# A fused attention and Fourier mixing kernel: column tiles, paired steps and folded tables on the Fourier side, one load a segment for the attention outputs, and a new order of the work

## The chip, the cores and the metric

The kernel runs on one core of a Trainium2 chip. The core has five engines with queues of their own: PE (TensorE, matrix multiplies, and PEld, its weight loads), DVE (VectorE), ACT (ScalarE), POOL (GpSimd) and SP (SyncE, which here only issues DMAs). PE reads SBUF and writes PSUM; ACT and DVE read PSUM; POOL does not in this kernel. Sixteen DMA engines move data between SBUF and HBM. The metric is the device time of one execution in microseconds, the median of several runs; less is better.

## What is computed

Two branches over the same x (2048 tokens, 640 columns, bf16), mixed by a gate per token:

```python
def _A_ref(x, wq, wk, wv, wo, beta):          # H = 32 heads of 20, 4 segments of 512
    ...
    for s in range(N):
        logits = jnp.einsum('bhqd,bhkd->bhqk', qs, ks) * scale + mask     # causal
        p = _softmax(logits, axis=-1)
        a_dot = jnp.einsum('bhqk,bhkd->bhqd', p, vs)
        pq = phi(qs)                           # phi(t) = t + 1 if t > 0 else exp(t)
        num = jnp.einsum('bhld,bhde->bhle', pq, M)
        den = jnp.einsum('bhld,bhd->bhl', pq, z)[..., None] + 1e-06
        o = g * (num / den) + (1.0 - g) * a_dot
        pk = phi(ks)
        M = M + jnp.einsum('bhld,bhle->bhde', pk, vs)
        z = z + jnp.einsum('bhld->bhd', pk)
    return o @ wo

def _B_ref(x, w_r, w_i):
    X = jnp.fft.rfft2(x.astype(jnp.float32), axes=(-2, -1))
    X = X * (w_r + 1j * w_i)
    return jnp.fft.irfft2(X, s=(S, D), axes=(-2, -1)).astype(jnp.bfloat16)

g = _sigmoid((x * gate_w).sum(-1, keepdims=True))
return g * a + (1 - g) * b
```

## The kernel before

**How it is put together.** `Kern.record` lists 2328 steps ("ops"), each with the buffers that it reads and writes, the engines that could run it, and a name. `Sched.schedule` then goes through `ORDER`, a tuple written out by hand in the file: every entry is twice a step's number, plus one if the step's second engine is to run it (for an eviction ACT first and DVE second, for an elementwise step DVE first and POOL second). Each engine's queue is the steps of that engine in this order. The durations and latencies in the class (`HOPS`, `COST`, `QUEUE`) serve to choose PSUM banks and DMA semaphores; at run time the engines are held only by semaphore waits, which `emit` derives from the steps' predecessors (`o.preds`) and from bank and semaphore reuse (`o.dyn`). SP's queue is in order: a DMA whose data isn't ready holds all behind it.

PSUM has eight banks: four for the logits (`qk`), taken together, and four (`gen`) for everything else.

**Attention side.** For each segment: xT is loaded transposed (`xt_load`, L883), q, k and v are projected, logits come in units for a pair of head groups (`qk_unit`, L1242), ACT takes the exponentials (L1278), POOL zeroes what lies above the diagonal (`mask`, L1296), and PE multiplies by v (`pv_flipped`, L1193, for segments 0 to 2; `pv_group`, L1304, for segment 3). For segments 0 to 2 the outputs go to a DRAM scratch `u_scr` and come back in `finish_tile` (L1522) as five loads `ld_u` of 128 KB a segment into `oU`; they are then multiplied by the reciprocal denominators (`normal`, which come back over `r_scr`), the memory part is added (`addmem`), and the output projection (`oproj`) runs in column tiles of 32 rows or in one piece, after whatever ran before on PE (`mode=-1`). Masks of one unit that belong to two groups are issued apart for each, 224 in all.

**Fourier side** (`fft`, L1381). The two-dimensional transform is written as matrix multiplies:

- `fold` (L906): x (16 tokens a partition) is folded along its 640 columns into even and odd halves, on DVE or POOL.
- F1: multiplies over the 128 partitions by `fcat`; the result `Ac` has 5 chunks of columns by 16 steps g of 128.
- For each step g: **D**, six matmuls with 128 columns of `Ac` as weights and the tables `big` streaming (161, 321 and 160 columns, twice), into two PSUM banks, evicted to `Bt` (`ev_D`). **T**: two banks of two matmuls each (tables `tt` as weights, 321 columns of `Bt` streaming). **W_mul** (L1455): DVE multiplies each bank with both parts of W into `Pt`, 642 elements. **W_add** (L1460): two adds of 321 elements make `Yt`, on DVE or POOL. **Tb**: six matmuls of 256 columns, weights `Yt`, into two banks, evicted to `Cp` (`ev_Tb`).
- Every second step, one load of 512 KB for `tt` and four of 80 KB for W (`ld_W`); both are double-buffered.
- **Db**: for each of 16 n2 and two types, three matmuls of 321 columns over `Cp`; one type is evicted to `eo` and the other added and subtracted by `sum_Db` (L1501) into `G`.

**End.** In `finish_tile`, for each tile of 128 tokens and each half of the columns, four matmuls by the gate table bring in `G` (`Fb`), `oproj` adds the attention part in the same bank, an eviction (`final`) and a store follow.

A matmul step has a tiling of the PE array, its `mode`: 0 is the whole array, 1 the logits' tiles (20 rows by 64 columns), 2 is four column tiles of 32 rows of output, which may stream different data, and -1 takes what stands. Matmuls are recorded on L529, or on L527 where an untiled one is split.

Of the kernel before, what the change touches and what calls it, by code (L numbers as in the profile page):

```python
# [8 lines left out]
ALU = mybir.AluOpType  # L9
# [6 lines left out]
H = 32  # L16
# [28 lines left out]
class Op:  # L45
    __slots__ = ("id", "alts", "preds", "succs", "prio", "banks", "nbytes", "npred", "eng", "t0", "t1",
                 "stamp", "need_inc", "dyn", "first", "outside", "name", "dma", "key", "xfer", "lock", "mode", "emode", "hold", "width")


class Sched:  # L50
# [6 lines left out]
    FREE, PORT, LATE = 52.0, (85.0, 55.0), 500.0  # L57
# [57 lines left out]
    COST = {(0, 1): 94.0, (0, 2): 94.0, (1, 0): 130.0, (1, 2): 130.0, (2, 0): 106.0, (2, 1): 100.0}  # L115

    def schedule(self, pools, order, nsem=56):
# [32 lines left out]
        two = False  # L150
# [24 lines left out]
        def head(e):  # L175
# [18 lines left out]
            if o.dma:  # L194
                gate = window()
                if gate is not None:
                    t = max(t, gate.t1 + self.HOPS[e]["dma"])
            if e == "dve" and o.lock:
                t = max(t, free["pool"] + (20.0 if two else -self.PORT[0]))
            elif e == "pool":  # L200
                t = max(t, port - self.PORT[1])
            return t

        while len(self.order) < len(order):
# [20 lines left out]
            free[e] = o.t1 = t + occ  # L225
            if e == "dve" and o.lock:
                port = t + occ
            if e == "pool":
                two = o.lock
            if o.dma:  # L230
                if o.hold:
                    free[e] = max(free[e], max(ring) + 170.0)
                for q in range(o.width):
                    ring[q] = max(ring[q], free[e] + 1300.0) + o.xfer
# [84 lines left out]
def make_tables():  # L319
# [12 lines left out]
    F, Fp = F.reshape(128, 128), Fp.reshape(128, 128)  # L332
# [20 lines left out]
    dd = np.arange(KD)  # L353
    IC = np.zeros((384, 322))
    IS = np.zeros((384, 322))
    IC[:KD, :KD] = ck[:, None] * np.cos(2 * pi * kd[:, None] * dd[None] / D)
    IS[:KD, :KD] = ck[:, None] * np.sin(2 * pi * kd[:, None] * dd[None] / D)
    IS[0] = 0
    IS[320] = 0
    IS[:, 320] = 0  # L360

    T = np.zeros((16, 128, 4, 128))
    Tp = np.zeros((16, 128, 2, 2, 16, 4, 2))
    n2 = np.arange(16)
    k2 = np.arange(16)
    for g in range(16):
        for half in range(2):
            for i in range(4):
                kb, pi_, kind, sg = pair_of(g, half, i)
                k = kb + 128 * k2  # L370
                ph = 2 * pi * np.outer(n2, k) / S
                c, s = np.cos(ph), np.sin(ph)
                m = half * 64 + k2 * 4 + i
                kr = n2 * 8 + pi_ * 2
                ki = kr + 1

                def put(t, rows, val):
                    T[g, rows[:, None], t, m[None, :]] = val
                if kind == "pair":
                    put(0, kr, c), put(0, ki, sg * s), put(1, kr, -s), put(1, ki, sg * c)  # L380
                    put(2, kr, -s), put(2, ki, sg * c), put(3, kr, -c), put(3, ki, -sg * s)
                else:
                    src = kr if kind == "zero" else ki
                    put(0, src, c), put(1, src, -s), put(2, src, -s), put(3, src, -c)

                def putp(r, typ, eo, val):
                    for q in range(16):
                        Tp[g, m[q], r, typ, :, pi_, eo] = val[:, q]
                if kind == "pair":
                    putp(0, 0, 0, c), putp(1, 0, 0, -s), putp(0, 0, 1, -sg * s), putp(1, 0, 1, -sg * c)  # L390
                    putp(0, 1, 0, -s), putp(1, 1, 0, -c), putp(0, 1, 1, -sg * c), putp(1, 1, 1, sg * s)
                else:
                    eo = 0 if kind == "zero" else 1
                    putp(0, 0, eo, c), putp(1, 0, eo, -s), putp(0, 1, eo, -s), putp(1, 1, eo, -c)

    def chunks(t):
        return np.ascontiguousarray(t.reshape(3, 128, -1).transpose(1, 0, 2))
    fcat = np.concatenate([F, np.eye(128), Fp], 1)
    inv = np.concatenate([chunks(IC), chunks(IS)], 1).reshape(128, 6 * 322)
    big = np.concatenate([dtab, inv], 1)  # L400
    hmask = np.zeros((128, 5, 8, VW))
    for t in range(5):
        for r in range(128):
# [3 lines left out]
            "tt": np.concatenate([T.reshape(16, 128, 512), Tp.reshape(16, 128, 512)], 2).astype(b),  # L407
            "hmask": hmask.reshape(128, 880).astype(b)}


def base_of(g, i):

    return (0, 32, 48, 16)[i] if g == 0 else (g, g + 32, 64 - g, 32 - g)[i]


def pair_of(g, half, i):

    if g == 0:
        if half == 0:
            return 32 * i, i % 2, ("zero", "pair", "nyq", "pair")[i], (1, 1, 1, -1)[i]  # L420
        return 16 + 32 * i, (3, 2, 2, 3)[i], "pair", (1, 1, -1, -1)[i]
    if half == 0:
        return g + 32 * i, i, "pair", (1, 1, -1, -1)[i]
    return 32 - g + 32 * i, 3 - i, "pair", (1, 1, -1, -1)[i]
# [48 lines left out]
class Kern:  # L473
# [10 lines left out]
    def b(self, *key):  # L484
        v = self.bufs.get(key)
        if v is None:
            v = self.bufs[key] = Buf(str(key))
        return v
# [23 lines left out]
    def mms(self, items, r, w, prio, name="", extra=0.0, mode=0):  # L512
# [18 lines left out]
        op = self.Sc.op({"pe": (f, cost, self.DRAIN.get(name, 141.0))}, r=r, w=w, prio=prio, name=name, mode=mode)  # L531
        return op
# [10 lines left out]
    def one(self, eng, fn, n, r, w, prio, per=None, fix=None, name="", after=()):  # L543
        fix0, per0, late = {"act": (65, 0.833, 110.0), "dve": (67, 1.04, 68.0), "pool": (132, 0.945, 50.0)}[eng]
        per = per0 if per is None else per
        fix = fix0 if fix is None else fix
        return self.Sc.op({eng: (fn, fix + per * n, late)}, r=r, w=w, prio=prio, name=name, after=after)
# [9 lines left out]
    def dma(self, dst, src, nbytes, r, w, prio, tr=False, name="", after=(), queue="sp"):  # L557
        def f(e):
# [3 lines left out]
            with self.nc.allow_non_contiguous_dma(reason="small strided loads"):  # L562
                return e.dma_start(d_, s_)
        cost, work, width = self.QUEUE[name] if name in self.QUEUE else self.QUEUE[name, nbytes]
        queues = ("sp", "act") if name in self.EARLY else (queue,)
        return self.Sc.op({e: (f, cost, 0.0) for e in queues}, r=r, w=w, prio=prio, nbytes=nbytes, name=name, after=after,
                          dma=True, xfer=work, hold=tr and nbytes > 500000, width=width)
# [3 lines left out]
        "ld_W": (620.0, 450.0, 16), "ld_beta": (400.0, 120.0, 16), "ld_big": (500.0, 2900.0, 16), "ld_den": (520.0, 150.0, 16),  # L571
        "ld_fcat": (400.0, 350.0, 16), "ld_g": (500.0, 1900.0, 16), "ld_gc": (580.0, 200.0, 16), "ld_gw": (420.0, 600.0, 16),
        "ld_hm": (600.0, 850.0, 16), "ld_r": (570.0, 700.0, 16), "ld_tt": (530.0, 1650.0, 16), "ld_u": (530.0, 600.0, 16),
        "ld_wka": (520.0, 1100.0, 16), "ld_wkb": (450.0, 1500.0, 16), "ld_wqa": (500.0, 1100.0, 16), "ld_wqb": (500.0, 2200.0, 16),
        "ld_wo": (600.0, 700.0, 16), "ld_wo2": (600.0, 3000.0, 16), "ld_wv": (450.0, 3000.0, 16), "ld_x": (450.0, 830.0, 16),
        "oT": (1300.0, 750.0, 16), "pad2": (370.0, 200.0, 10), "pad": (400.0, 1250.0, 10), ("pkT", 131072): (1260.0, 600.0, 16), ("pkT", 262144): (1280.0, 1100.0, 16),
# [1046 lines left out]
```

## Time and profile before

Three runs took 243.2, 249.15 and 241.87 us, median 243.2. The profiled execution took 240.85 us; its span, first to last instruction, is 238.9, and the remaining 1.95 lie around it. The granted PE clock is 0.998 on average.

| group of instructions | count | busy us | mean ns |
|---|---|---|---|
| ACT exponentials `ex<-psum` L1278 | 92 | 138.7 | 1508 |
| POOL masks `ex<-ex` L1299 | 224 | 122.0 | 567 |
| DVE W_mul `Pt<-psum,Wt` L1455 | 32 | 25.6 | 822 |
| PE D `psum<-big,Ac` | 96 | 18.1 | 258 |
| PE Db `psum<-big,Cp` | 96 | 18.0 | 302 |
| PE Tb `psum<-tt,Yt` | 96 | 16.5 | 276 |
| PE T `psum<-Bt,tt` | 64 | 13.3 | 302 |
| SP issues of W loads, 80 KB each | 32 | | |
| SP issues of `oU<-u_scr`, 128 KB each | 15 | | |

Busy time is the time in which at least one instruction of a group runs, and the mean is that of one instruction from start to end. Matmuls overlap, so for PE a group's busy time is far under count times mean, and the time from one matmul's start to the next is shorter still than the busy time suggests. DVE, ACT and POOL run one instruction after another, so there busy time is work.

### The profile page before, as it was taken

Reading aid. Unit: us, or ns where it says so; the run is one execution under the profiler, and the core shown is the slowest. Engines: PE = TensorE matmul, PEld = TensorE weight load, DVE = VectorE, ACT = ScalarE, POOL = GpSimd, SP = SyncE. Lnnn points to the kernel's source line nnn. Section 1 sums busy time; section 2 is a strip of 40 time slices with the busy share of each in tenths; the row PEclk is TensorE's granted clock in tenths of the full one; section 3 lists DMA queues with packets and bytes.
Section 4 is the critical chain, followed back from the end, with each engine's and each line's share of the span. In section 5 each row is a group of like instructions: output and inputs, shape, how many; then the busy total and the mean of one; then the engine's idle time right before and its main releaser. Section 6 shows DMA issues by size and latency. Waiting matters only on the chain.

```text
span 238.9 us, 10255 instructions
## 1 busy us (share of the span) xinstructions
PE 227.6 (95%) x4361; PEld 140.1 (59%) x4361; DVE 196.6 (82%) x481; ACT 199.5 (83%) x241; POOL 166.7 (70%) x297
## 2 busy tenths in 40 slices
PE   7899999999999999999989999999999999899994
PEld 2575566775456566555646655455645466567794
DVE  0579998889899996898999798997988896846563
ACT  2189688898899999999999979999899988797730
POOL 8523268457969956937974999875889868678730
PEclk9999999999999999999999999999999999999999
DMA  7999849996996876483779572364766995872223
GB/s 171 277 366 233 231 125 185 264 207 149 250 227 158 153 210 178 110 241 72 237 213 261 171 226 62 103 157 144 204 205 162 244 215 83 121 107 83 59 86 111
DMA packets 58928, 42.17 MB, mean 177 GB/s; under 512 B 30020, under 2 KB 55172, under 8 KB 58884
## 3 DMA queue, kind: packets, MB, share of 16 engines
q1 hardware_dynamic: 57844, 40.96, 69.9%
q8 instruction: 34, 0.56, 1.0%
q10 hardware_dynamic: 1040, 0.57, 0.8%
q14 instruction: 10, 0.08, 0.2%
HBM read 23.32 MB, written 12.30 MB: 149 GB/s over the span
## 4 chain that ended last, share of the span: by engine, by line
PE 54%; DVE 19%; ACT 14%; DMA 7%; issue 3%; SPq 1%; DVEq 0%
PE psum L529 48%; ACT ex L1278 9%; PE psum L527 6%; DVE Pt L1455 3%; DMA r_scr<-rc 3%; ACT et L1087 2%; DMA xT<-in_A_x_dram 2%; DMA Wt<-in_B_w_i_dram 2%; DVE xsb L921 2%; DVE xf L916 2%; DVE G L1501 1%; DVE va L1130 1%; DVE q L540 1%; DMA r<-r_scr 1%; DVE oU L1542 1%
## 5 line engine op out<-in xcount | busy, mean ns | idle before, releaser
L1278 ACT ACTIVATE ex<-psum 128x2048 bf16<-128x2048 f32 (+4 forms) x92 | 138.7, 1508 | 12.2 <-PE psum L529 10.1
L1299 POOL TENSOR_SCALAR_AFFINE_SELECT ex<-ex 128x256 bf16<-128x256 bf16 (+2 forms) x224 | 122.0, 567 | 37.2 <-ACT ex L1278 33.7
L529 PE MATMUL psum<-qkp 20*64 20x64 bf16 (+5 forms) x1280 | 32.3, 270 | 2.2 <-ACT ex L1278 2.0
L529 PE MATMUL psum<-xT,wk 128*128 128x256 bf16 (+1 forms) x280 | 33.9, 273 | 0.2
L529 PE MATMUL psum<-xT,wq 128*128 128x512 bf16 (+1 forms) x135 | 30.7, 380 | 0.8 <-DMA xT<-in_A_x_dram 0.8
L529 PE MATMUL psum<-wv,xT 128*32 128x321 bf16 (+3 forms) x400 | 30.0, 301 | 0.3 <-DVE va L1130 0.3
L1455 DVE TENSOR_TENSOR Pt<-psum,Wt 128x642 bf16<-128x642 f32 x32 | 25.6, 822 | 2.2 <-PE psum L529 1.9
L529 PEld LDWEIGHTS psum<-qkp 20*64 20x64 bf16 x1280 | 13.3, 102 | 19.7 <-ACT ex L1278 15.4
L529 PEld LDWEIGHTS psum<-xT,wk 128*128 128x128 bf16 (+1 forms) x280 | 19.9, 97 | 6.5 <-DMA wk<-in_A_wk_dram 0.6
L527 PE MATMUL psum<-wo,oU 128*32 128x320 bf16 x480 | 21.9, 300 | 0.7 <-DVE oU L1550 0.5
L921 POOL TENSOR_TENSOR xsb<-xf 128x320 bf16<-128x320 bf16 (+2 forms) x12 | 9.5, 790 | 16.1 <-DVE xsb L921 12.4
L529 PEld LDWEIGHTS psum<-wv,xT 128*32 128x32 bf16 (+1 forms) x400 | 14.6, 96 | 7.5 <-issue 2.6
L1130 DVE TENSOR_TENSOR va<-psum,ebx 128x320 bf16<-128x320 f32 x32 | 15.2, 484 | 4.4 <-ACT gate L1128 2.1
L529 PE MATMUL psum<-big,Ac 128*128 128x160 bf16 (+2 forms) x96 | 18.1, 258 | 0.4 <-DVE Pt L1455 0.3
L529 PE MATMUL psum<-big,Cp 128*128 128x321 bf16 (+1 forms) x96 | 18.0, 302 | 0.2 <-DVE G L1501 0.2
L529 PE MATMUL psum<-ex,va 128*32 128x64 bf16 (+3 forms) x576 | 17.4, 257 | 0.4 <-DVE mem L1175 0.2
L1501 DVE TENSOR_TENSOR G<-eo,psum 128x320 bf16<-128x320 f32 x32 | 14.7, 483 | 3.6 <-PE psum L529 2.6
L540 DVE CAST ot<-psum 128x320 bf16<-128x320 f32 x21 | 10.1, 491 | 9.1 <-PE psum L527 5.9
L529 PE MATMUL psum<-tt,Yt 128*128 128x256 bf16 (+1 forms) x96 | 16.5, 276 | 0.5 <-DVE Yt L1460 0.2
L529 PEld LDWEIGHTS psum<-ex,va 128*32 128x32 bf16 x576 | 10.8, 96 | 9.6 <-POOL ex L1299 1.3
L1087 ACT ACTIVATE et<-qu 128x512 bf16<-128x512 bf16 x25 | 15.6, 631 | 0.2
L527 PEld LDWEIGHTS psum<-wo,oU 128*32 128x32 bf16 x480 | 11.9, 96 | 5.4 <-issue 1.4
(99 smaller groups left out, 392.7 us busy)
## 6 DMA issues: line engine op xcount, KB each, us to landing
qkp<-qk_scr SPq DMA_DIRECT2D x28, 160.0 KB
tt<-tab_tt SPq DMA_DIRECT2D x8, 512.0 KB, 4.5
qk_scr<-qu SPq DMA_DIRECT2D x12, 256.0 KB, 3.1
u_scr<-ub SPq DMA_DIRECT2D x12, 256.0 KB, 3.7
xsb<-in_A_x_dram SPq DMA_DIRECT2D x8, 320.0 KB, 6.5
oU<-u_scr SPq DMA_DIRECT2D x15, 128.0 KB, 2.9
out_dram<-ot SPq DMA_DIRECT2D x12, 160.0 KB
Wt<-in_B_w_r_dram SPq DMA_DIRECT2D x16, 80.2 KB, 2.6
```

The source lines that it names most:

```text
L527: h = e.matmul(dst, wt, r_, start=st, stop=sp_, **{**kw, "tile_position": (0, q), "skip_group_check": True})
L529: h = e.matmul(o_, l_, r_, start=st, stop=sp_, **kw)
L540: alts["dve"] = (lambda e: e.tensor_copy(dst(), src()), 67 + 1.04 * n, 68.0)
L916: self.either(lambda e, r=r, op=op: e.tensor_tensor(xf.ap(r * 642, [321, 2], [1, 320]), xs.ap(o, [D, 2], [1, 320]), xs.ap(o + 320, [D, 2], ...
L921: self.either(lambda e, dst=dst, src=src, d0=d0, n=n, op=op: e.tensor_tensor(xs.ap(o + dst, [D, 2], [1, n]), xf.ap(src + d0, [321, 2], [1, ...
L1087: self.one("act", lambda e: e.activation(et.ap(0, [1, L]), qsl(), ACT.Exp), L, [qb], [b("et", pi_)], late, fix=95, name="phi_exp")
L1130: self.one("dve", lambda e: e.tensor_tensor(va.ap(i * H * VW + h0 * VW, [VW, nh], [1, DH]), self.ps(bank, 0, [DH, nh], [1, DH]), self.ebx. ...
L1278: self.one("act", lambda e, d=d, q=q: e.activation(self.ex.ap(*d), self.ps(bank, *q), ACT.Exp, scale=SC), n, [bank], [self.exb(s, 2 * pr + ...
L1299: self.one("pool", lambda e: e.affine_select(self.ex.ap(e0 + d0, [1280, 4], [1, n], np_=np_), self.ex.ap(e0 + s0, [1280, 4], [1, n], np_=np_),
L1455: self.one("dve", lambda e, ri=ri, Pt=Pt, Wt=Wt, wo_=wo_, bank=bank: e.tensor_tensor(Pt.ap(ri * 322, [644, 2], [1, KD]), self.ps(bank, 0, ...
L1501: self.one("dve", lambda e, q=q, n2=n2, bank=bank, eo=eo: e.tensor_tensor(self.G.ap(n2 * D + 639 * q, [1 - 2 * q, 320]), eo.ap(q, [1, 320] ...
L1542: self.either(lambda e, c=c: e.tensor_tensor(oT.ap(c * L, [1, L]), oT.ap(c * L, [1, L]), self.r4[s].ap(0, [1, L]), ALU.mult), L, [b("r4", ...
```

## The change

- **D** runs in column tiles (`mode=2`): one bank holds, for 64 columns of `Ac`, the cosine part in partitions 0 to 63 and the sine part in 64 to 127; a step still streams 1284 columns' worth over the four tiles, in 24 matmuls. `base_of`, `start_of` and `row_of` give the new order of the rows; `ev_F1` writes `Ac` in runs of 4.
- **T** contracts over all 128 rows at once, so one pass of 321 columns by four column tiles makes a bank, for two steps g together.
- **Steps in pairs**: eight pairs instead of sixteen steps. `W_add` takes 642 elements; `Z_fold` is new: it adds and subtracts the mirrored halves of `Yt` into `Zt` (644 and 640 elements, one operand read backwards). `Pt` and `Yt` are single-buffered, `Zt` double.
- **Tb** works with 64 rows for each step of a pair, in two row tiles (`mode=3`, new), 128 columns a matmul, into two banks.
- **Folded tables**: `Db` streams 161, 321 and 160 columns instead of three times 321, and `sum_Db` writes every second element. `big` shrinks from 805 to 644 KB and each `tt` load from 512 to 256 KB. W comes in 8 loads of 40 KB a pair.
- **Loads**: x in 4 loads of 640 KB instead of 8 of 320; xT of segments 1 to 3 in three pieces; `oU` in one load of 640 KB a segment, with 5 KB in a row, and `wo` rows in the matching order.
- **Masks** of the two groups of a unit are joined where their buffers lie next to each other: 33 fewer.
- **Order**: `ORDER` is replaced, and 2328 steps become 2293. In `Sched`, the durations of DMAs, the fetching of PE's instructions and the port that DVE and POOL share are modelled otherwise; of this only one line adds waits: a POOL step waits for the locked DVE step that stands ahead of it.

The core of the diff:

```diff
@@ Sched.schedule
             if e == "dve" and o.lock:
                 port = t + occ
+                ldv = o
             if e == "pool":
-                two = o.lock
+                if ldv is not None:
+                    o.dyn.append(ldv)
+                two, ldv = o.lock, None
...
+D_PARTS = (((0, 160, 161, 0), (1, 0, KD, 162), (2, 0, 160, 484)), ((2, 0, 160, 644), (3, 0, KD, 804), (4, 160, 161, 1126)))
+DB_PARTS = (((0, 0, 161, 0), (1, 0, KD, 162), (2, 161, 160, 484)), ((0, 161, 160, 644), (1, 0, KD, 804), (2, 0, 161, 1126)))
...
+def start_of(g, X, h):
+
+    return ((0, 32), (16, 48))[X][h] if g == 0 else ((g, 64 - g), (g + 32, 32 - g))[X][h]
...
@@ fft
-        for g in range(16):
...
+        for pr in range(8):
...
+            for r, wd in enumerate((self.wr_d, self.wi_d)):
+                for h in range(4):
+                    row, row1 = (start_of(2 * pr + h // 2, X, h % 2) for X in range(2))
...
+            for g in (2 * pr, 2 * pr + 1):
+                Bt = self.Bt[g % 2]
+                for X in range(2):
+                    bank = Bank(1, "gen")
...
+                    for n_, parts in enumerate(zip(*D_PARTS)):
+                        items = []
+                        for h in range(4):
+                            def th(h=h, n_=n_, part=parts[h // 2], g=g, X=X, bank=bank):
+                                c, c0, n, tc = part
+                                return (self.ps(bank, c0, [1, n], p0=32 * h, np_=32), self.Ac.ap(c * 2048 + g * P + X * 64 + h % 2 * 32, [1, 32]), big.ap(tc, [1, n]),
+                                        n_ == 0, n_ == 2, {"tile_position": (0, 32 * h), "skip_group_check": True})
...
+            for X in range(2):
+                for ri in range(2):
+                    bank = Bank(1, "gen")
+                    items = []
+                    for h in range(4):
+                        def th(ri=ri, X=X, h=h, tt=tt, bank=bank):
+                            return (self.ps(bank, 0, [1, KD], p0=32 * h, np_=32), tt.ap(h // 2 * 256 + X * P + ri * 64 + h % 2 * 32, [1, 32]),
+                                    self.Bt[h // 2].ap(X * 322, [1, KD]), True, True, {"tile_position": (0, 32 * h), "skip_group_check": True})
...
+                self.either(lambda e, r=r, a0=a0, a1=a1, op=op: e.tensor_tensor(
+                    Yt.ap(r * 644, [322, 2], [1, KD]), Pt.ap(a0, [644, 2], [1, KD]), Pt.ap(a1, [644, 2], [1, KD]), op), 2 * KD, Pb,
+                    [b("Yt", 2 * r), b("Yt", 2 * r + 1)], prio2, after=self.after_q0(("Yt", r)), name="W_add")
+            Yb = [b("Yt", i) for i in range(4)]
+            for q, (n, op) in enumerate(((161, ALU.add), (160, ALU.subtract))):
+                self.either(lambda e, q=q, n=n, op=op, Zt=Zt: e.tensor_tensor(
+                    Zt.ap(161 * q, [322, 4], [1, n]), Yt.ap(0, [322, 4], [1, n]), Yt.ap(320, [322, 4], [-1, n]), op), 4 * n,
+                    Yb, [b("Zt", i2, q)], prio2, after=self.after_q0(("Zt", i2, q)), name="Z_fold")
...
+                    for X in range(2):
+                        for r in range(2):
+                            for g in range(2):
+                                def th(c=c, X=X, g=g, r=r, np_=np_, n_=n_, Zt=Zt, tt=tt, bank=banks[g]):
+                                    return (self.ps(bank, X * n_ * P + c % 2 * P, [1, P], np_=np_), Zt.ap((2 * r + X) * 322 + c * P, [1, np_], p0=64 * g, np_=64),
+                                            tt.ap(512 + X * 256 + r * P, [1, P], p0=64 * g, np_=64), r == 0, r == 1, {"tile_position": (64 * g, 0), "skip_group_check": True})
...
@@ finish_tile
+                    self.dma(lambda c0=c0, n=n: oT.ap(c0 * L, [1, n * L]),
+                             lambda c0=c0, n=n: dap(self.ud.ap(), (s * 1024 + c0) * L, [32 * L, H], [5 * L, 4], [1, n * L]),
+                             P * n * L * 2, [b("ud", s, i) for i in range(4)], ob[c0:c0 + n], prio - 8.0, name="ld_u", after=home)
-                    self.dma(lambda c=c: oT.ap(c * L, [1, L]), lambda c=c: dap(self.ud.ap(), (s * 1024 + 4 * c) * L, [32 * L, H], [L, 4], [1, L]),
-                             P * L * 2, [b("ud", s, i) for i in range(4)], [ob[c]], prio - 8.0, name="ld_u", after=home)
```

359 lines of the change are left out of this document (193 added, 166 removed), and 193 rows, old and new, of the table ORDER.

## The prediction

> **What bounds the kernel now.** I read the engines' totals and the chain of waits first, then the stretches, then single groups. Totals and chain, from the page of the profile:
>
> ```profile
> span 238.9 us, 10255 instructions
> ...
> PE 227.6 (95%) x4361; PEld 140.1 (59%) x4361; DVE 196.6 (82%) x481; ACT 199.5 (83%) x241; POOL 166.7 (70%) x297
> ...
> PE 54%; DVE 19%; ACT 14%; DMA 7%; issue 3%; SPq 1%; DVEq 0%
> ```
>
> PE carries most of the chain, but its 95% is not all work, because a matmul counts as busy until its last result is out while the next already runs. The timeline (start, duration, engine, line, form, count) gives the real pace:
>
> ```profile
> 60.41 0.73 PE L529 MATMUL psum<-ex,va 128*32 128x512 bf16 x24
> ...
> 130.35 0.61 PE L529 MATMUL psum<-tt,Yt 128*128 128x256 bf16 x4
> ...
> 131.72 0.43 PE L529 MATMUL psum<-qkp 20*64 20x512 bf16 x12
> ```
>
> The middle row: the four start 0.11 us apart, 4 x 256 columns in 0.44 us, 0.42 ns a column (the rest of 0.61 is the last one's latency). The first row: 24 matmuls of 32 output rows; each of the four column tiles gets 512+384+192+3x64 = 1280 columns, 0.53 us at that pace, plus 0.19 of latency: the four tiles run side by side. The last row does so in eight tiles. Costing all 4361 matmuls so (columns x 0.417 ns, over 4 or 8 where tiled, plus 2.5 ns for an untiled one and 0.8 for a tiled one) gives 185.5 us of column time. PE also changes tiling 229 times in the trace, and the start after a change comes a median 97 ns late: 22.2 us. So PE works 207.7 us and waits 31.2. By stretches (PE, PEld, DVE, ACT, POOL busy, clock, DMA share):
>
> ```profile
> 80.00:100.00 20.00, 19.89 (x352) 11.93 (x351) 17.05 (x37) 19.16 (x23) 14.42 (x27) 1.00 0.73 174
> 100.00:120.00 20.00, 19.42 (x325) 11.23 (x324) 18.56 (x46) 19.51 (x24) 14.57 (x30) 1.00 0.63 177
> 140.00:160.00 20.00, 19.07 (x298) 10.20 (x294) 18.45 (x37) 18.80 (x21) 17.95 (x32) 1.00 0.42 115
> ```
>
> ACT is 94 to 98% busy there and DVE 85 to 93%; PE does 15.1 to 17.2 us of column time and some 1.9 of tiling changes per 20. Three engines are near full and wait for each other, so a gain on PE lands only in part.
>
> **PE, part by part.** Columns before, for the 16 steps: D 6 matmuls, 1284 columns a step; T 1284; Tb 1536; Db 32 x 963.
> - D: four column tiles of 32 rows, 1284 columns a step as before; 8.6 us both ways, 0.
> - T: one pass of 321 columns by four tiles where two full passes stood; 8 pairs x 1284 columns fewer = 10272 x 0.417 = -4.3 us.
> - Tb: 64-row tiles, two side by side; 8 x 1536 columns fewer = -5.1 us. No row of before shows a 64-row, 128-column tile. Ends: 0 if they don't overlap, -5.1 if they do; the nearest row is the eight-tile one above, which overlaps, so -5.1.
> - Db: folding halves two of three passes, 32 x 321 columns fewer = -4.3 us.
> - Tiling changes: counted in the two order lists (an entry is twice a step's number, plus one for its second engine), 220 become 262; 42 x 97 ns = +4.1. Into and out of the new tiling the delay isn't shown; from 0 to the 411 ns that 1 in 10 of the changes to the logits' tiling exceed, those including other waits; 97 taken.
>
> Net 13.7 - 4.1 = 9.6 us less PE work (range 4.5 to 13.7).
>
> Against this speaks the number of weight loads, 96 to 384 in D:
>
> ```profile
> L529 PEld LDWEIGHTS psum<-big,Ac 128*128 128x128 bf16 x96 | 8.1, 97 | 5.3 <-DVE Pt L1455 1.2 <-DVE Macc L1372 0.5 <-issue 0.4
> ...
> L529 PEld LDWEIGHTS psum<-ex,va 128*32 128x32 bf16 x576 | 10.8, 96 | 9.6 <-POOL ex L1299 1.3 <-DVE Pt L1455 0.7 <-DVE Cp L540 0.7
> ```
>
> A load of 32 columns lasts as long as one of 128, but 24 of them went by within the 0.73 us above, behind the streaming; 0 taken, and up to 288 x 96 ns = 27.7 us if that cover were gone. The Trainium skill, "TensorEngine Tiling (Array Packing)", Restrictions, says that column tiling switches the fast weight load off. The equal 96 and 97 ns agree with it; by that rule alone the sum would be as much as 27.7 us worse, and the 0.73 us row decides against that.
>
> **DVE, ACT, POOL.** The rows (busy, mean ns):
>
> ```profile
> L916 DVE TENSOR_TENSOR xf<-xsb 128x640 bf16<-128x640 bf16 x15 | 7.5, 515 | 1.2 <-DMA xsb<-in_A_x_dram 1.1
> L916 POOL TENSOR_TENSOR xf<-xsb 128x640 bf16<-128x640 bf16 x1 | 1.4, 1401 | 0.0
> L1460 POOL TENSOR_TENSOR Yt<-Pt 128x321 bf16<-128x321 bf16 x16 | 11.7, 734 | 1.0 <-DVE Pt L1455 0.5 <-PE psum L529 0.4 <-DVE gg L1011 0.2
> L1460 DVE TENSOR_TENSOR Yt<-Pt 128x321 bf16<-128x321 bf16 x16 | 5.8, 385 | 0.0
> ```
>
> - W_mul stays 32 x 0.82 us; the evictions of F1, D, Tb and Db keep their counts and sizes.
> - W_add becomes 16 of 642 (13 DVE, 3 POOL by the list): DVE 13 x 0.485 (the quartile of the 640 row) = 6.3 against 6.2, POOL 4.2 against 11.7.
> - Z_fold is new, 10 on DVE (+4.9) and 6 on POOL (+8.4). Its reversed operand has a row, the folds of xsb, 320 reversed elements in a median 0.32 us, so it is no dearer.
> - The list moves 10 folds from POOL to DVE (+3.9, -7.9), 2 gate tables to POOL (-1.6, +2.3), and net evictions off DVE onto ACT (-3.3; ACT +2.0).
> - 33 of 224 masks go by joining: 11 x (2 x 0.26 + 0.24) = -8.4 us of POOL. Other POOL moves +1.5.
> - The stride-2 writes of sum_Db: 0 to 32 x 40 ns = +1.3 (ev_D writes so, 522 ns for 322 against 481 for 321 plain); 0 taken.
> - New wait: a POOL step waits for the locked DVE step ahead of it in the order; behind it stand masks, and the PV matmuls wait for those (1.3 us in five waits now). Price: 0 to 164 locked DVE steps x 0.4 us = 66 us of POOL waiting, under its 72 us idle. In return, 36 DVE steps now last longer than the median of their form, 9.6 us together, by up to 0.56 each. I take half back, -4.8.
>
> DVE: +4.9 + 0.1 + 3.9 - 1.6 - 3.3 = +4.0, -0.8 with the waits; ACT +2.0; POOL -12, which is on no piece of the chain and counts 0.
>
> **DMA and SP.** SP's issues last 157.8 us in sum. W loads go from 32 to 64 (0.67 us each, +21.5), ld_u 15 to 3 (12 x 0.59, -7.1), x loads 8 to 4 (-1.8), three xT loads (4.2 to 6.1 us each) become nine (1.2 to 1.3 each, as the first three now), -4.3. SP stays under three quarters full. tt halves (2 MB less of 42). Two DMA pieces stand on the chain in order of time (start, us):
>
> ```profile
> 150.14 4.20 DMA Wt<-in_B_w_i_dram
> ...
> 192.74 6.70 DMA r_scr<-rc
> 199.46 2.26 DMA r<-r_scr
> ```
>
> PE worked beside both. From 145 to 155 it did 7.2 us of columns where the neighbours' pace gives 7.9, from 190 to 205 9.9 against 11.7: with its tiling changes that is 3.3 us lost. A new order and one ld_u per segment move both; 0 to -3.3, and I take -2. The first matmul waits for an xT that SP issues behind an x load (0.41 us); the new list puts all three first: -0.5, between 0 and -1.
>
> **The sum.** What leaves an engine shortens the chain about by that engine's share of it: PE -13.7 x 0.54 = -7.4, tiling changes +4.1 x 0.54 = +2.2, DVE -0.8 x 0.19 = -0.2, ACT +2.0 x 0.14 = +0.3, stalls -2.0, start -0.5: -7.6. The profiled execution took 240.85 us (238.9 of span and 1.95 around it), so 233.2. The median shown, 243.2, is 1.0% above that execution; at the same distance 235.5. Between them, 234.
>
> **Rivals.**
> 1. All of it lands: PE -9.6 in full, stalls -3.3, start -1, so 227. For it: PE is the commonest thing that ACT and DVE wait for. Against: ACT would need 97% from its first exponential to its last, its best stretch now. 0.10.
> 2. PSUM reading is the bound: ACT and DVE together are busy 396.1 us and idle 81.7 in two spans. With +6.0 and the idle kept, the span is (402.1 + 81.7)/2 = 241.9, time 244. For it: the stretches above. Against: much of that idle is waiting for PE. 0.13. The Trainium skill, same page, PSUM Bottleneck, has this as a rule: tiling speeds up the matmuls and not the reading of their results. The unchanged counts of evictions and W_mul agree with it.
> 3. Slower: W comes late. Each pair needs nine issues on the in-order SP where it needed five, each behind stores that wait for their data; a pair without its W stops W_mul, W_add, Z_fold and Tb for both steps. The one stall of before cost 4.65 us of chain; at four of eight pairs 4 x 4.65 = 18.6, so 234 + 18.6 = 253. It decides from three stalled pairs (248). For it: 32 more issues. Against: loads can go a pair ahead, two W buffers as now. 0.09.
> 4. It doesn't do what it says: Tb's tiles don't overlap and tiling changes cost double: 5.1 x 0.54 + 2.2 = 5 us back, 239. 0.06.
>
> **Numbers.** The forecast has 0.62, with a range of its own of 229 to 239. The range 226 to 244 takes in rivals 1, 2 and 4 and leaves out rival 3 and the ends. A measurement of this kernel tells some 2% from no change, so 238.3 and 248.1 part the cases. Faster: 0.59 of the forecast, rival 1, a third of rival 4 and part of rival 2: 0.73. Slower: rival 3, 0.09. Within: 0.18.
>
> **What would show it.** T at one pass of 321 columns per four matmuls, Tb's pairs starting together, PE column time near 172 us; tiling changes near 260; DVE's total near 196 and fewer stretched steps; no W transfer on the chain; the first projection starting before 7.8 us. Wrong if ACT or DVE take over PE's share of the chain at an unchanged span (rival 2), or if W or Z_fold stand on it (rival 3).

## The result, and the profile after

The changed kernel is slower: a median of 249.2 us (247.9 to 251.3, 4 runs) against 244.4 us of the kernel before beside it on the same chip, a ratio of 1.027, 95% interval 1.020 to 1.034. The profiled execution took 247.9 us, with a span of 246.2.

The page's totals and its chain of waits:

```profile
span 246.2 us, 11186 instructions
...
PE 218.8 (89%) x4793; PEld 134.3 (55%) x4809; DVE 195.2 (79%) x487; ACT 202.0 (82%) x246; POOL 157.2 (64%) x253
...
PE 20%; ACT 6%; POOL 3%; DVE 3%; issue 1%
```

PE's total fell by 8.8 us, DVE's by 1.4 and POOL's by 9.5, and ACT's rose by 2.5, yet the span is 7.3 us longer. The chain's shares sum to a third because it could be followed back only to 160 us; they are not comparable with those of before.

The timeline has the new forms of T, Tb and D (start, duration, engine, line, form, count):

```profile
59.09 0.32 PE L574 MATMUL psum<-Bt,tt 128*32 128x321 bf16 x4
...
112.55 0.62 PE L574 MATMUL psum<-tt,Zt 64*128 64x128 bf16 x16
...
97.88 0.46 PE L574 MATMUL psum<-big,Ac 128*32 128x161 bf16 x12
```

T's four tiles of 32 columns go by in 0.32 us where 321 columns alone last 0.30: they run side by side. Tb's 16 matmuls are 2048 columns, 0.85 us at 0.417 ns each; they go by in 0.62 us, which is half of 0.85 plus the 0.19 of latency, so its two row tiles run side by side too. D's twelve matmuls last as long as its three did before:

```profile
83.16 0.46 PE L529 MATMUL psum<-big,Ac 128*128 128x161 bf16 x3
```

Some groups (busy, mean ns, idle before and its releaser): two of PE's weight loads, then the DVE groups that wait for DMAs:

```profile
L574 PEld LDWEIGHTS psum<-ex,va 128*32 128x32 bf16 x576 | 11.6, 98 | 11.7 <-POOL ex L1357 4.9 <-issue 0.9 <-DVE Bt L586 0.4
...
L574 PEld LDWEIGHTS psum<-big,Ac 128*32 128x32 bf16 x384 | 7.5, 95 | 9.1 <-DVE qu L586 2.9 <-issue 1.9 <-DVE Pt L1513 1.1
...
L1513 DVE TENSOR_TENSOR Pt<-psum,Wt 128x642 bf16<-128x642 f32 x32 | 25.2, 818 | 3.1 <-DMA Wt<-in_B_w_i_dram 1.9
...
L586 DVE CAST qu<-psum 128x512 bf16<-128x512 f32 x16 | 10.8, 683 | 4.7 <-DMA qk_scr<-qu 3.5
```

By stretches of 20 us (columns as before: PE, PEld, DVE, ACT, POOL busy, clock, DMA share, GB/s):

```profile
60.00:80.00 20.00, 17.16 (x335) 9.21 (x336) 16.61 (x44) 17.05 (x19) 13.35 (x26) 0.91 0.83 160
80.00:100.00 20.00, 19.44 (x443) 11.52 (x429) 18.18 (x46) 18.98 (x22) 15.95 (x25) 1.00 0.57 157
100.00:120.00 20.00, 16.56 (x344) 8.65 (x333) 17.24 (x36) 16.61 (x18) 11.50 (x20) 1.00 0.54 138
120.00:140.00 20.00, 17.50 (x408) 11.33 (x412) 17.97 (x53) 17.96 (x19) 15.33 (x24) 1.00 0.71 153
140.00:160.00 20.00, 18.11 (x449) 8.95 (x442) 18.47 (x37) 18.72 (x20) 16.42 (x29) 1.00 0.64 175
```

Two stretches stand out, 60 to 80 and 100 to 120: there PE, DVE and ACT fall together, ACT to 17.05 and 16.61, where before had 19.16 and 19.51. Three engines that idle more at once suggest a wait for something that is none of them. The granted clock of 0.91 is half speed from 65.6 to 69.1 us; another run at a mean of 1.000 took 248.3 us, so that is not what makes the kernel slow. The exponentials of the logits serve as milestones, 92 in both kernels. The tenth starts 2.2 us earlier than before, the 16th 1.1 later, the 34th 3.9 later, the 46th 5.2 later, and from there to the last the lag stays between 5.0 and 6.1. So the loss is made between 50 and 140 us. The milestones also say where. From the 12th to the 14th the kernel loses 2.4 us, and there W comes late (SP's issue of the last two loads of the first pair, then W_mul):

```profile
58.20 1.22 SPq L609 DMA_DIRECT2D Wt<-in_B_w_i_dram  x2
...
61.88 1.56 DVE L1513 TENSOR_TENSOR Pt<-psum,Wt 128x642 bf16<-128x642 f32 x2 [1.91 <-DMA Wt<-in_B_w_i_dram]
```

From the 28th to the 29th it loses 1.3 us, behind a store:

```profile
97.96 0.49 SPq L609 DMA_DIRECT2D qk_scr<-qu  x1
98.50 0.60 SPq L609 DMA_DIRECT2D Wt<-in_B_w_r_dram  x1
99.14 0.59 SPq L609 DMA_DIRECT2D Wt<-in_B_w_i_dram  x1
99.78 0.58 SPq L609 DMA_DIRECT2D qk_scr<-qu  x1
100.41 2.22 SPq L607 DMA_TRANSPOSE xT<-in_A_x_dram  x1
...
103.20 0.69 DVE L586 CAST qu<-psum 128x512 bf16<-128x512 f32 x1 [2.19 <-DMA qk_scr<-qu]
...
103.95 0.10 PEld L574 LDWEIGHTS psum<-big,Ac 128*32 128x32 bf16 x4 [1.78 <-DVE qu L586]
```

A store of queries stands behind two W loads on SP, which take 1.3 us; DVE idles 2.19 us until the store has landed and the buffer is free, and PE's next D waits 1.78 us for DVE. From 90.3 to 103.9 us SP issued without a break of more than 0.1 us, nine W loads among 17 issues. In the last five of these microseconds SP of the kernel before twice issued nothing, for 1.5 and 1.0 us.

### The profile page after: what moved, and what is told of

Same layout as the page of the kernel before. It is cut to its first block, busy times and chain, and to the rows that moved or that the text cites. A ratio compares the mean times of both kernels' runs of the same rounds, so it can differ in the third digit from the quotient of the medians.

```text
span 246.2 us, 11186 instructions
## 1 busy us (share of the span) xinstructions
PE 218.8 (89%) x4793; PEld 134.3 (55%) x4809; DVE 195.2 (79%) x487; ACT 202.0 (82%) x246; POOL 157.2 (64%) x253
## 5 line engine op out<-in xcount | busy, mean ns | idle before, releaser
L1357 POOL TENSOR_SCALAR_AFFINE_SELECT ex<-ex 128x256 bf16<-128x256 bf16 (+3 forms) x191 | 115.8, 625 | 53.2 <-ACT ex L1331 15.5
L574 PE MATMUL psum<-wv,xT 128*32 128x321 bf16 (+3 forms) x400 | 30.8, 301 | 0.1
L574 PE MATMUL psum<-xT,wq 128*128 128x512 bf16 (+1 forms) x119 | 26.3, 380 | 2.6 <-DMA xT<-in_A_x_dram 0.9
L574 PEld LDWEIGHTS psum<-qkp 20*64 20x64 bf16 x1280 | 13.4, 103 | 18.8 <-ACT ex L1331 12.4
L574 PE MATMUL psum<-ex,va 128*32 128x64 bf16 (+3 forms) x576 | 18.1, 261 | 3.4 <-POOL ex L1357 3.1
L574 PE MATMUL psum<-big,Ac 128*32 128x321 bf16 (+2 forms) x384 | 16.6, 260 | 3.0 <-DVE qu L586 2.3
L574 PEld LDWEIGHTS psum<-ex,va 128*32 128x32 bf16 x576 | 11.6, 98 | 11.7 <-POOL ex L1357 4.9
L574 PEld LDWEIGHTS psum<-xT,wq 128*128 128x128 bf16 (+1 forms) x135 | 9.3, 97 | 10.2 <-issue 2.0
L574 PE MATMUL psum<-big,Cp 128*128 128x321 bf16 (+4 forms) x96 | 13.5, 258 | 1.4 <-DVE G L1566 0.9
L586 DVE CAST qu<-psum 128x512 bf16<-128x512 f32 x16 | 10.8, 683 | 4.7 <-DMA qk_scr<-qu 3.5
L586 DVE CAST ot<-psum 128x320 bf16<-128x320 f32 x15 | 7.2, 489 | 8.3 <-PE psum L572 5.4
```

The lines of the kernel that those rows point to most:

```text
L574: h = e.matmul(o_, l_, r_, start=st, stop=sp_, **kw)
L586: alts["dve"] = (lambda e: e.tensor_copy(dst(), src()), 67 + 1.04 * n, 68.0)
L1357: self.one("pool", lambda e: e.affine_select(self.ex.ap(e0 + d0, *dims, np_=np_), self.ex.ap(e0 + s0, *dims, np_=np_), [[0, 4 * pair], [st ...
```

## The experiments

Ratios are to runs of the kernel before on the same chip, with 95% intervals.

**The W loads.** *e1*, the changed kernel with 32 W loads of 64 partitions instead of 64 of 32. It reads as many bytes, but other rows of W than the steps need, and in runs of 1284 bytes.

```diff
-                for h in range(4):
-                    row, row1 = (start_of(2 * pr + h // 2, X, h % 2) for X in range(2))
...
+                for h in range(0, 4, 2):
+                    def half(Wt_=Wt, r=r, h=h, wd=wd, row=2 * pr + h // 2):
+                        self.dma(lambda: Wt_.ap(r * 644, [KD, 2], [1, KD], p0=32 * h, np_=64),
+                                 lambda: dap(wd, row * KD, [32 * KD, 64], [KD, 2], [1, KD]), 128 * KD * 2, [],
...
```

> The changed kernel with W in 32 loads of 80 KB instead of 64 of 40 KB, the same bytes, at the place in the order of the earlier of the two that each replaces; the rows are taken from other places of W, so the output differs. Theory A (SP's queue is overfull from 40 to 160 us, some 18.3 of each 20 us, so W and the stores of q and k come late): SP falls by about 21 us in sum, the stalls of DVE for W (1.9 us) and for the stores out of qu (3.5) go, time about 243 to 245. Theory B (POOL's new waits) and theory C (PE was not the bound): 248 to 250, as the changed kernel.

Measured: 243.6 us, ratio 1.002 (0.997 to 1.007). SP's issues sum to 145.9 us instead of 171.4. The same stretches of e1:

```profile
60.00:80.00 20.00, 18.68 (x416) 10.06 (x419) 19.59 (x56) 19.36 (x22) 16.06 (x31) 1.00 0.76 166
...
100.00:120.00 20.00, 18.18 (x405) 9.36 (x406) 19.45 (x48) 19.29 (x22) 13.82 (x22) 1.00 0.60 128
```

ACT and DVE are back at 19.3 to 19.6 of 20. The 16th exponential starts 2.5 us before that of the kernel before (the changed kernel's 1.1 after), and the gap between e1 and the changed kernel opens at the two places above: it is 0.1 us at the 12th, 1.9 at the 14th, 3.6 at the 16th, 3.7 at the 28th and 5.7 at the 29th and the 46th. Between the 14th and the 16th lies the halved clock; e12 and e14 (below), where W_mul waits for W at the same place, show it there too, e1 and e17 do not. Of the three waits of DVE for W and for stores of queries, two are gone and one is left:

```profile
DVE qu L597 <- DMA qk_scr<-qu: 1.7, 1, 1.7
```

It comes at 130 us, where the changed kernel has one of 1.3 us at 136, so that one is not owed to the doubled loads. So the doubled loads make the slowdown. What is left without them is a tie and not the predicted gain.

*e4*, the kernel before with each W load cut into two of 32 partitions, one right behind the other.

```diff
-                        self.dma(lambda r=r, Wt=Wt, h=h, slot=slot, step=step: Wt.ap(r * 644 + slot * KD, [step * KD, 2], [1, KD], p0=64 * h, np_=64),
...
+                        for k in range(2):
+                            o = self.dma(lambda r=r, Wt=Wt, h=h, slot=slot, step=step, k=k: Wt.ap(r * 644 + slot * KD, [step * KD, 2], [1, KD], p0=64 * h + 32 * k, np_=32),
...
```

> The kernel before with each W load split into two of 40 KB, issued one behind the other: 64 instead of 32, the same bytes. Theory A: SP's sum rises from 158 to about 178 us, W and stores come late, 247 to 252. Theory B and C: 244, no change.

Measured: 244.8 us, ratio 1.005 (1.001 to 1.009), SP's sum 170.3 us, and none of these waits of DVE. The same number of issues costs some 1 us in the old order, short of theory A's 247 to 252, and 6 in the new one. From 40 to 140 us SP issues for 75 us in the kernel before, 82 in e4, 87 in the changed kernel and 70 in e1.

*e14*, the changed kernel with W loads behind the next five other transfers of SP's queue.

```diff
+            if o.name == "ld_W":
+                self.nw += 1
+                if (self.nw - 1) // 8 in (0, 3, 4, 5, 6):
+                    late.append([v, 5])
+                    continue
+            moved.append(v)
```

> The changed kernel with all its 64 W loads, those of step pairs 0, 3, 4, 5 and 6 moved behind the next five other transfers of SP's queue (their last load was issued 11 to 18 us before the first multiplication by W). Theory place (W loads cost by standing ahead of the stores of the queries and the pads): most of the 6 us comes back, 243.5 to 246 us, ratio to before 1.00 to 1.015, and the wait of DVE for the stores of the queries (3.5 us) goes under 1.5. Theory number (64 issues on SP cost wherever they stand): no change, ratio 1.02 to 1.035.

Measured: 256.4 us, ratio 1.058 (1.052 to 1.063), worse than both theories said. The expectation had a false premise: it gave the loads to the pairs in the sequence of issue, but in the order list the loads of neighbouring pairs interleave. By the list, the last load of pairs 0, 2, 3, 5 and 7 is issued only 3.1 to 5.8 us before the pair's first W_mul, and that of pairs 1, 4 and 6 11 to 13 us before. So loads that were just in time became late, as the waits (us in total, times, longest) and the timeline say:

```profile
DVE Pt L1529 <- DMA Wt<-in_B_w_i_dram: 5.4, 2, 3.2
...
DVE Pt L1529 <- DMA Wt<-in_B_w_r_dram: 3.2, 1, 3.2
```

```profile
112.53 0.59 SPq L625 DMA_DIRECT2D Wt<-in_B_w_r_dram  x1
...
114.80 1.56 DVE L1529 TENSOR_TENSOR Pt<-psum,Wt 128x642 bf16<-128x642 f32 x2 [3.16 <-DMA Wt<-in_B_w_r_dram]
```

The run says nothing for number against place, but it shows that SP's queue has little slack: earlier W loads hold up stores, later ones hold up W_mul. (e15, with ten other transfers in place of five, gave no result: in that order the queues wait for one another in a ring.)

*e16*, *e17*, *e18*: all 64 loads and the output kept, half of them (W's imaginary part) issued by POOL, half by ACT, and all by POOL. In e16 and e18 POOL's loads also get eight DMA semaphores of their own, out of those that SP had. The line of e17:

```diff
-                             [b("Wt", i2, r, h)], early, name="ld_W")
+                             [b("Wt", i2, r, h)], early, name="ld_W", queue="act" if r == 1 else "sp")
```

> The changed kernel with the 32 loads of W's imaginary part issued by POOL instead of SP; same sizes, same places in the order, same output. Theory issuer (SP's in-order issue is what was short): SP is relieved of 22 us, as in the run with 32 loads, which had a ratio of 1.002: 243 to 246 us, ratio 0.995 to 1.015, less whatever POOL pays for issuing (no trace shows a load issued by POOL; POOL is busy 157 of 246 us). Theory transfer (small loads are slow whoever issues them): no gain, 1.02 to 1.035. POOL as a bad place for it (its masks are late): above 1.04.

> The same 32 loads issued by ACT (its own four output stores at the end took 0.39 to 0.45 us of ACT each, so about 14 us of ACT, which is busy 202 of 246 us). Theory issuer: gains 4 to 6 us on SP's side and pays a part of the 14 us on ACT's: 246 to 252, ratio 1.01 to 1.04. Theory transfer: only the price, 250 to 262, ratio 1.03 to 1.08.

> All 64 W loads issued by POOL. Theory issuer: SP falls from 171 to 128 us of issuing, and the stores of the queries never stand behind a W load: 238 to 244, ratio 0.98 to 1.005, if POOL's price is hidden. Theory transfer: 1.02 to 1.035. POOL as a bad place: above 1.04.

Measured: e16 262.7 us, ratio 1.078 (1.072 to 1.084); e17 249.2 us (its runs 245.2 to 252.8), 1.020 (1.012 to 1.028); e18 285.3 us, 1.169 (1.162 to 1.177). An issue took a median 0.55 us on POOL and 0.58 on ACT. POOL is the bad place that the third theory feared. What this did to the rest in e18 (waits, as above):

```profile
PEld psum L573 <- POOL ex L1356: 35.8, 18, 6.0
PE psum L573 <- POOL ex L1356: 30.0, 14, 5.7
```

In the changed kernel the first of these is 5.5 us. POOL's masks of the exponentials stand behind W loads, with 36.0 us of issuing and 13.9 of waiting ahead of it, and PV waits for the masks. e17 is the telling one: with 18.7 us more on ACT its 16th exponential starts 2.4 us before that of the kernel before (the changed kernel's is 1.1 after), so taking issues off SP does win back the first stall. In it DVE waits neither for W nor for a store of queries, though the loads are as many and as small. By the 46th it is 2.4 us after (the changed kernel 5.2); that ACT's extra work cost it again fits, but is not shown apart. Its ratio lies inside the issuer theory's 1.01 to 1.04 and below the transfer theory's 1.03 to 1.08, and its interval overlaps the changed kernel's own (1.020 to 1.034). The Trainium skill, "Perfetto Trace Analysis", DMA Optimizations, says that spreading transfers over the engines that can issue them may help where issuing is the bottleneck. In these runs it won nothing on the whole: the other queues belong to engines whose own work waits behind the loads. The granted clock of e14, e16 and e18 was lower as well (0.956, 0.957 and 0.925 in the profiled runs, 0.993 in the changed kernel); what of their time is owed to that is not shown.

**POOL's wait.** *e2*, the changed kernel without the new wait, and *e5*, the kernel before with it.

```diff
-                if ldv is not None:
-                    o.dyn.append(ldv)
```

> The changed kernel without the added wait of a POOL step for the locked DVE step ahead of it. Theory B: PE's waits for masks fall from 8.9 us back towards the 1.3 of the kernel before, time 244 to 246, though some DVE steps grow longer again (9.6 us in sum before). Theory A and C: 248 to 250; if the wait does what it is for, slower than 250.

> The kernel before with the changed kernel's added wait alone: a POOL step waits for the locked DVE step ahead of it in the order. From the run without it (DVE steps stretched by 22.6 us in sum instead of 5.1, 16.6 us more DVE, 10 us slower): the 9.6 us that 36 DVE steps are stretched by before fall to about 4, time 239 to 242. If the wait only suits the new order, because the old one doesn't lead POOL's steps up to it: 245 to 250, with PE waiting for masks.

Measured: e2 259.9 us, 1.068 (1.059 to 1.077); e5 242.3 us, 1.001 (0.997 to 1.005). The totals of e2:

```profile
PE 223.9 (86%) x4793; PEld 136.2 (52%) x4809; DVE 211.8 (82%) x487; ACT 201.9 (78%) x246; POOL 161.7 (62%) x253
```

Without the wait 43 of the changed kernel's DVE steps exceed the median of their form by more than 60 ns, by 22.6 us together; with it 19 steps do, by 5.1. PE's waits for masks fall from 8.9 to 3.9 us, so the wait has a price, and it is worth more than its price. In the old order it changes nothing: 32 stretched steps, 9.9 us, which neither expectation had. The wait is worth some 10 us in the new order, and nothing by itself. e2's granted clock was lower too (0.964 in the profiled run), so how much of the 10 us comes from the longer DVE steps alone is not shown.

**Is any engine's work the bound?** Six runs shorten the work of the kernel before, each leaving something out: *e3*, the second half of each T and Tb sum and half of two passes of Db (13.7 us of PE's column time); *e7*, W_mul on 161 of 321 columns (DVE 6.9 us less by the totals); *e8*, the exponentials of phi on 128 of 512 columns (ACT 7.8 us less); *e9*, those three together; *e10*, 48 exponentials of the logits on 448 of 512 columns (10.4 us); *e13*, e10 with e3.

```diff
-                        return (self.ps(bank, 0, [1, KD]), tt.ap(to + (2 * ri + q) * P, [1, P]), Bt.ap(q * 322, [1, KD]), q == 0, q == 1, {})
+                        return (self.ps(bank, 0, [1, KD]), tt.ap(to + (2 * ri + q) * P, [1, P]), Bt.ap(q * 322, [1, KD]), True, True, {})
...
-                    Pt.ap(ri * 322, [644, 2], [1, KD]), self.ps(bank, 0, [0, 2], [1, KD]), Wt.ap(wo_, [644, 2], [1, KD]), ALU.mult), 2 * KD,
+                    Pt.ap(ri * 322, [644, 2], [1, KD if g < 2 else 161]), self.ps(bank, 0, [0, 2], [1, KD if g < 2 else 161]),
+                    Wt.ap(wo_, [644, 2], [1, KD if g < 2 else 161]), ALU.mult), 2 * KD,
...
-            self.one("act", lambda e: e.activation(et.ap(0, [1, L]), qsl(), ACT.Exp), L, [qb], [b("et", pi_)],
+            self.one("act", lambda e, n=L if self.phc < 2 else 128: e.activation(et.ap(0, [1, n]), qt.ap(qo, [1, n]), ACT.Exp), L, [qb], [b("et", pi_)],
...
-            outs = [((e0 + 576 * kind, [1280, 4], [1, 512]), (0, [512, 4], [1, 512]))]
+            full = 512 if s * 8 + g < self.NEX + 1 else 448
+            outs = [((e0 + 576 * kind, [1280, 4], [1, full]), (0, [512, 4], [1, full]))]
```

> The kernel before, order and all other work unchanged, with 13.7 us of PE column time left out: T without its second pass, Tb without its second row part, Db with 161+321+160 columns instead of 3 x 321; the output differs. Prediction's step (what PE is relieved of lands by its share of the chain, 54%): 244.4 - 7.4 = 237. Theory C (ACT and DVE are the bound, PE waits longer instead): 242 to 245.

> The kernel before, order unchanged, with W_mul on 161 of 321 columns in all steps but the first two, about 28 x 0.33 = 9.3 us less DVE; the output differs. Theory C (the evicting engines are the bound): 239 to 242. If DVE waits as PE does, and ACT alone sets the pace: 243 to 245.

> The kernel before, order unchanged, with the exponential of phi on 128 of 512 columns in all but the first two, about 28 x 0.35 = 10 us less ACT; the output differs. Theory C with ACT as the bound: 235 to 238. With DVE as the bound, or with each engine waiting for the next in the given order: 242 to 245.

> The kernel before with all three reliefs, 13.7 us of PE, 9.3 of DVE and 10 of ACT; the output differs. If ACT alone is the bound: as the run with ACT's relief. If the engines limit one another, more than the sum of the three single gains: 230 to 236. If the order or SP and the DMAs hold it: 241 to 244.

> The kernel before with 48 of the 56 large exponentials of the logits written over 448 instead of 512 columns of each of their four heads (64 columns of each keep older values): 48 x 256 columns x 0.833 ns = 10.2 us less on ACT, about the 8 us that the three-quarters shorter phi exponentials took from ACT without any gain. Theory loop (the pace is a ring of one set of four PSUM banks: logits matmuls fill them, the exponential empties them, and the next logits can't start before it ends, so 138.7 us of exponentials and the hand-over between them set the time while the rest fills the gaps): 8 to 10 us faster, ratio 0.96 to 0.967. Theory order (every engine follows its own fixed queue and no ring is tighter than another): at most 1 us, ratio 0.995 to 1.0, as with the other reliefs.

> The kernel before with both the shorter exponentials and the 13.7 us of PE column time left out (second half of each T pair and Tb pair, two thirds of Db in part). Theory loop: the ring still leads, so the same time as with the shorter exponentials alone or up to 2 us less. Theory 'PE behind the ring': if PE is the next bound once the ring is shorter, the PE relief is now worth 3 us or more beyond the shorter exponentials alone.

| run | ratio | 95% interval |
|---|---|---|
| e3, PE | 1.001 | 0.997 to 1.006 |
| e7, DVE | 0.996 | 0.992 to 0.999 |
| e8, ACT (phi) | 0.998 | 0.995 to 1.002 |
| e9, all three | 1.004 | 1.000 to 1.007 |
| e10, ACT (logits) | 1.019 | 1.014 to 1.024 |
| e13, ACT (logits) and PE | 0.994 | 0.990 to 0.999 |

The best gains 0.6% where 24 us of work are gone. Three of e3's runs had a mean granted clock of 1.000 and took 241.9 to 242.8 us, against 243.1 before, so a slower clock does not hide a gain of 7 us there. e7 and e8 alone decide little: by the shares of the chain DVE's 6.9 us would give 1.3 and ACT's 7.8 would give 1.1, within what the intervals allow. e3 and e9 decide. In e9 the totals did fall:

```profile
PE 217.3 (90%) x4268; PEld 133.2 (55%) x4281; DVE 191.1 (79%) x481; ACT 191.4 (79%) x241; POOL 166.5 (69%) x297
```

and the waits took it up: PE's weight loads wait 20.7 us for the exponentials (15.4 before), the exponentials 17.5 us for PE (10.1 before).

```profile
PEld psum L529 <- ACT ex L1278: 20.7, 52, 1.0
ACT ex L1278 <- PE psum L529: 17.5, 35, 1.6
```

That looked like one ring, logits to exponential to free banks to logits, and e10 tests it. The ring theory fell: 10.4 us out of the ring itself gave nothing, and the whole run was 4.6 us slower, which the other theory (at most 1 us faster) did not have either. Up to the 76th exponential e10 runs 1.7 us behind the kernel before, and it loses another 4.4 by the 82nd, in a stretch where the granted clock of its profiled run is 0.74 (the column after POOL):

```profile
200.00:220.00 20.00, 17.41 (x403) 10.74 (x403) 10.91 (x28) 12.13 (x14) 10.38 (x17) 0.74 0.56 88
```

Before, it was 1.00 there. Other runs of e10 with a mean granted clock of 0.993 were as slow (245.8 and 247.6 us), so the clock isn't all of it; the rest stays open. In e13 both reliefs together put the 70th exponential 3.3 us earlier, of 24 us taken out, and the end 1.4. Its PE relief is worth 6 us beyond e10 (1.019 to 0.994), over the 3 us set for 'PE behind the ring'; but e10 is itself slower than the kernel before, so this settles nothing. What fits all six is that several chains of nearly one length run through the fixed order, so that shortening one or two only lengthens waits. That is what remains, not something a run has shown by itself.

*e12*, the changed kernel with e10's shorter exponentials:

> The changed kernel with the same 48 exponentials written over 448 columns. Theory loop with W loads that stall it: the loads stay, so about the same 8 to 10 us come off the changed kernel's 249: 239 to 241, ratio to before 0.985 to 0.995. If the waits on SP's queue have become the bound throughout (a queue of transfers that can't go faster), shorter exponentials give nothing: ratio 1.02 to 1.03.

Measured: 248.8 us, 1.019 (1.014 to 1.025), level with the changed kernel. Its stalls are not shortened by less work on ACT either: DVE waits 1.8 us for W and 2.9 and 1.7 for the two stores.

## Why the prediction was wrong

Most sizes were right, and the way from sizes to time was wrong, at two places.

- **PE's work.** Column time, costed as in the prediction, comes to 168.4 us for the matmuls recorded and 3.5 for 16 whose records are missing: near 172, as foreseen. There are 269 tiling changes for some 260, with the 64-row tiles counted as a tiling of their own. From one matmul's start to the next, waits included, T fell from 10.6 to 6.8 us (3.8 for 4.3), Db from 17.1 to 12.4 (4.7 for 4.3) and Tb from 13.5 to 9.7 (3.8 for 5.1). D was put at 0 and rose from 12.1 to 16.2. That is not its streaming: where D's matmuls run without another between them, twelve mostly take 0.45 to 0.47 us (14 of 19 times) and three took 0.44 to 0.46 (8 of 9). Of the 4.1 us, 2.0 are more idle time behind D's matmuls, and ten more tiling changes right behind them make an estimated 1.0 at the 97 ns of before; the last us is not explained. Its weight loads are hidden, as predicted: 95 ns each, with twelve within those 0.46 us.
- **DVE, ACT, POOL.** 195.2 us for 196, 202.0 for 201.5, 157.2 for about 155. The half taken back from stretched steps (4.8 us) is 4.5: 9.6 to 5.1. The new wait's price on POOL's side was counted as nothing; it is there (PE waits 8.9 us for masks, 3.9 without the wait), but with it the kernel is 10 us faster than without.
- **The failed step: "What leaves an engine shortens the chain about by that engine's share of it".** It booked -7.4 us for PE's 13.7. In e3 the same 13.7 us of column time left out gave a ratio of 1.001 (0.997 to 1.006), so this term was 0. In e9 the shares would give 9.8 us for 13.7 of PE, 6.9 of DVE and 7.8 of ACT; the ratio was 1.004 (1.000 to 1.007). A share of the chain says which work happened to end last at each instant, not what remains of the chain when that work is gone; with three engines at 85 to 98% and tied to each other, another chain of the same length may stand beside it; no run shows that chain. e3 and e9 keep the old order. In the new one only the whole is measured: with W loads back at 32 (e1) the change is a tie, which fits this term at 0 and the small ones with it.
- **The failed cover: "SP stays under three quarters full".** This put SP's term at nothing. Over the whole span it is true (171.4 of 246.2 us, 70%). Where the loads stand it is not: SP was issuing 18.2 to 18.5 of 20 us in 20 to 60, 80 to 100 and 120 to 140, and 17.8 in 60 to 80. Before, it issued 18.5 in 20 to 40 and 14.1 to 16.7 from 40 to 140. e1 prices the doubled loads: 6 us, ratio 1.027 to 1.002. A full queue alone is not the price, since e4 has 170.3 us of issuing and costs 1; what stands where in the new order counts too.
- **Rival 3** named the right queue and half of the victims, at a chance of 0.09. It had W arrive late and W_mul wait in four of eight pairs. W came late in one pair, for 1.9 us; there e1 and the changed kernel part by 1.8 us up to the 14th exponential and by 3.5 up to the 16th. What the rival did not have is the transfers behind the loads: a wait of 2.2 us for a store of queries, where they part by 2.0 more, with PE and ACT idle beside it. The time was 249 and not 253. e14 made the rival's mechanism larger, with 8.6 us of waits for W and 256 us.
- **Rival 2** (the reading of PSUM as the bound, 244) falls: in e9 DVE and ACT have 13.6 us less to do, which by its sum is 6.8 us, and the time stays. e1's 243.6 us is its number without its mechanism.
- **Rivals 1 and 4.** Nothing landed in full, and Tb's tiles do overlap, so both fall.
- **Start and stalls.** The first exponential starts 2.4 us earlier (10.9 for 13.3), more than the 0.5 booked. The twelfth is still 2.5 us ahead; then the W loads take it.

Still open is how the 6 us divide between SP's time to issue and the transfers' own size, since e1 changed both, and the rows of W besides. e17, which changed only the issuer, is level with e1 at the 16th exponential, so the first stall is a matter of SP's queue; it then falls behind e1 again, by 2.9 us at the 46th. Where e1's own lead of 2 us goes after the 40th exponential is open too, but for the store at 130 us.

## What to carry to other kernels

Before a saving is booked, take the work out and see whether the time moves: in a kernel whose order was fitted to its durations, 7 to 14 us of work less on one engine were worth some 1 us at most. Count the issues on an in-order DMA queue by stretches and not over the span, and look at what stands right behind each added one, and at how long before its use the last one lands. An issue of 0.6 us had no free place to go here: on ACT or POOL it stands ahead of work that others wait for.

## What the runs showed of the hardware

- DVE steps run long when POOL works beside them, and how long hangs on the order: 22.6 us over 43 steps without the wait, 5.1 over 19 with it, beside a difference of 10 us in time. Each of these steps, and each of the 36 of the kernel before, starts while a POOL step runs.
- A load of 40 KB costs each of its three issuers about the same: a median of 0.60 us on SP, 0.58 on ACT and 0.55 on POOL. The Trainium skill, "SBUF — State Buffer", SBUF: two separate sides, warns that a transfer issued by POOL can stall because DVE locks it out of the shared port; in e16 and e18 the loads landed a median 2.6 and 3.2 us after issue, 3.1 from SP in the changed kernel, so here the loads were not late and the masks behind them were.
- Less work can come with a lower granted clock: 0.74 from 200 to 220 us in e10, 0.91 in e13, 1.00 before. In both it is half speed for a stretch, 10.2 us from 206.4 on and 3.4 us from 200.5 on.
